# Part B: Q and K for 32 rows on four column tiles, 8 heads at a time, only V and Wo streamed

## The chip, the cores and the metric

The kernel runs on one core of a Trainium2 chip (trn2). The metric is the device time of one execution in microseconds. The core has five engines, each with its own instruction queue: TensorE (PE in the profile; PEld is its weight load), VectorE (DVE), ScalarE (ACT), GpSimd (POOL) and SyncE (SP), which only issues DMAs here. Sixteen DMA engines move data between DRAM and the on-chip SBUF; matmuls write to PSUM, from where DVE or ACT copy results to SBUF.

## The reference

Two independent computations share one launch; their outputs stand side by side in the last axis of the result. Everything is bf16.

Part A is a local attention with 32 heads of 20 over 2048 tokens of width 640: every token attends to 8 earlier tokens at a distance of 2. The change leaves it alone.

Part B is a recurrent memory transformer: 2048 tokens in 64 segments of 32, and 8 memory tokens in front of each. The output rows of the memory tokens are the memory of the next segment, so segments run one after another.

```python
for s in range(n_seg):                       # 64 segments, one after another
    xs = x[:, s * 32:(s + 1) * 32, :]
    h = concatenate([mem, xs], axis=1)       # 40 tokens x 640
    q = einsum('btd,dhe->bhte', h, Wq)       # 32 heads x 192
    k = einsum('btd,dhe->bhte', h, Wk)
    v = einsum('btd,dhe->bhte', h, Wv)
    scores = einsum('bhqe,bhke->bhqk', q, k) * scale
    p = softmax(where(mask, scores, -1e9))
    o = einsum('bhqk,bhke->bhqe', p, v)
    o = einsum('bhte,hed->btd', o, Wo)
    mem = o[:, :8, :]
    outs.append(o[:, 8:, :])
```

Each of Wq, Wk, Wv and Wo is 640 x 6144 or its transpose: 61,440 bytes on each of 128 SBUF partitions, 245,760 for all four, which is more than fits.

## The kernel before

**Order.** `part_b` first loads some of its weights (L235), runs part A (`mid`, L236) while these arrive, then loads more resident weights (L249) and runs 64 calls of `segment`. TensorE's instructions in these keep the order in which the program writes them (`manual_schedule`, L457). The other engines' orders come from the tile framework, which also puts in the waits.

**Weights.** A unit is a piece of a weight matrix. For Q, K and V it is 128 rows of the 640 times 1024 columns, 256 KB (`(m, c, dc)`, c from 0 to 5, dc from 0 to 4); for Wo it is 256 of the 6144 rows, 320 KB. `weight_plan(161000)` picks the 75 units that stay in SBUF, spread over the segment's order so that the other 39 (29 of Q, K and V, 10 of Wo; 10.9 MB) are streamed in evenly again in every segment. `get_unit` (L251) streams one: it takes the next of 8 buffers (`b_ws`) and issues the load on SP. SP issues in program order, and waits at each load until the buffer's last reader has finished.

**A segment.** `HT` holds the segment's 40 tokens, transposed: 128 partitions x 5 pieces of the 640 x 64 columns, of which 40 are used. `project` (L298) multiplies it with 1024 weight columns: for each dc two matmuls with 64 stationary columns and 512 moving columns, on two column tiles of the array (tile positions (0, 0) and (0, 64)), so their results lie on PSUM partitions 0 to 63 and 64 to 127. `project_qk` copies the result to SBUF (`sb`), and one step later its `turn` (L312) brings it back to "feature x token" by four matmuls against a selection matrix and copies it to QT or KT. That happens 6 times for Q and 6 times for K. `evacuate` (L281) gives copies out of PSUM to ACT and DVE in turns.

Heads go in two halves of 16 (t2 = 0, 1): `scores` (L322: 32 matmuls, then the softmax on DVE and ACT), `turn_p` (L352: P transposed), `values` (V stays "token x feature", so it needs no turn), `mix` (L365: P times V, 32 matmuls per half), and `project_out` (L382: 48 units of two matmuls into one accumulator `Y`). Projections stand between the steps of a half, so that softmax and copies of one step lie beside TensorE's work of another. `prep` (L285) loads the next segment's 32 tokens of x (issued on POOL) and transposes them into the other `HT`. At the end (L439 to L451) Y is copied to `Ysb` by ACT, its memory rows are transposed by TensorE and copied into the next `HT` by DVE; the next segment's first projection waits for that. Two DMAs on POOL write the output rows (L453).

Of the kernel before, what the change touches and what calls it, by code (L numbers as in the profile page):

```python
# [7 lines left out]
FP32 = mybir.dt.float32  # L8
# [141 lines left out]
def head_pieces(h):  # L150
    i = h // 2
    if h % 2 == 0:
        return [(3 * i, 0, 128), (3 * i + 1, 0, 64)]
    return [(3 * i + 1, 64, 128), (3 * i + 2, 0, 128)]


def out_units():

    return [j for t2 in range(2) for gv in range(2) for j in range(12 * t2, 12 * t2 + 12) if (j // 2) % 2 == gv]


def weight_plan(budget):

    steps = []
    for t2 in range(2):
        for m in "qk":
            for c in range(3 * t2, 3 * t2 + 3):  # L170
                steps += [((m, c, dc), 0.245) for dc in range(5)]
        steps.append((None, 1.0))
    for c in range(6):
        steps += [(("v", c, dc), 0.216) for dc in range(5)]
        if c >= 2:
            steps.append((None, 0.5))
    steps.append((None, 0.6))
    for n, j in enumerate(out_units()):
        steps.append((("o", j, 0), 0.27))
        if n == 5:  # L180
            steps.append((None, 1.1))
    steps.append((None, 1.5))
    size = lambda u: 2560 if u[0] == "o" else 2048
    total = sum(size(u) for u, _ in steps if u)
    span = sum(t for _, t in steps)
    to_stream = total - budget
    now, done, streamed = 0.0, 0, []
    for u, t in steps:
        now += t
        if u is not None and done + size(u) / 2 <= to_stream * now / span:  # L190
            streamed.append(u)
            done += size(u)
    units = [u for u, _ in steps if u]
    while total - done > budget:
        u = next(u for u in reversed(units) if u not in streamed)
        streamed.append(u)
        done += size(u)
    return [u for u in units if u not in streamed]


def part_b(ctx, tc, B_x, B_mem0, B_Wq, B_Wk, B_Wv, B_Wo, out, ident, n_seg, budget, pre, nbuf, mid):
# [7 lines left out]
    wo_v = B_Wo.rearrange("h e d -> (h e) d").rearrange("(cc p) d -> p cc d", p=128)  # L209

    def unit_src(u):
        m, c, dc = u
        if m == "o":
            return wo_v[:, 2 * c:2 * c + 2, :]
        return w_in[m][:, dc, 1024 * c:1024 * c + 1024]

    def unit_shape(u):
        return [128, 2, 640] if u[0] == "o" else [128, 1024]

    resident = weight_plan(budget)  # L220
# [3 lines left out]
    def load_resident(pool, units):  # L224
        for k, u in enumerate(units):
            t = pool.tile(unit_shape(u), BF16, name="wres_%s%d_%d" % u)
            res_engs[k % 2].dma_start(t[:], unit_src(u))
            res[u] = t[:]

    n_pre, used = 0, 0  # L230
    while n_pre < len(resident) and used < pre:
        used += 2560 if resident[n_pre][0] == "o" else 2048
        n_pre += 1
# [17 lines left out]
    def get_unit(u):  # L251
        if u in res:
            return res[u]
        t = wstream.tile([128, 1280], BF16, tag="ws")
        v = t[:].rearrange("p (a n) -> p a n", a=2) if u[0] == "o" else t[:, 0:1024]
        nc.sync.dma_start(v, unit_src(u))
        return v
# [11 lines left out]
    QTs = [cpool.tile([128, 24 * L + PADW], BF16, name=f"QT{t2}") for t2 in range(2)]  # L269
    KTs = [cpool.tile([128, 24, L], BF16, name=f"KT{t2}") for t2 in range(2)]  # L270
    Ps = [cpool.tile([128, 8 * L + PADW], BF16, name=f"P{t2}") for t2 in range(2)]
    OTs = [cpool.tile([128, 12 * L + PADW], BF16, name=f"OT{q}") for q in range(4)]
# [4 lines left out]
    sel = ident.rearrange("p (g t) -> p g t", g=2)[:, :, 0:L]  # L277
# [7 lines left out]
    def prep(s):  # L285
        HT = HTs[s % 2]
        xr = one.tile([L, Dm], BF16, tag="xr")
        lo = 0 if s == 0 else M
        n = L - lo
        if s == 0:  # L290
            nc.gpsimd.dma_start(xr[0:M, :], mem2[0:M, :])
        nc.gpsimd.dma_start(xr[M - lo:L - lo, :], x2[SEG * s:SEG * s + SEG, :])
        pt = ps_tr.tile([128, 5, L], BF16, tag="tr")
        for dc in range(5):
            nc.tensor.transpose(pt[:, dc, lo:L], xr[0:n, dc * 128:(dc + 1) * 128], ident[0:n, 0:n])  # L295
        nc.scalar.copy(HT[:, :, lo:L], pt[:, :, lo:L])

    def project(HT, m, c):  # L298
        ps = ps_acc.tile([128, 512], FP32, tag="acc")
        for dc in range(5):  # L300
            w = get_unit((m, c, dc))
            for g in range(2):
                nc.tensor.matmul(ps[64 * g:64 * g + 64, :], lhsT=HT[:, dc, :], rhs=w[:, 512 * g:512 * g + 512],  # L303
                                 start=(dc == 0), stop=(dc == 4), tile_position=(0, 64 * g))
        return ps

    def project_qk(HT, m, c):
        ps = project(HT, m, c)
        sb = qk_sb.tile([128, 512], BF16, tag="sb")
        evacuate(sb[:], ps[:])  # L310

        def turn():  # L312
            pt = ps_tr.tile([128, 4, 2, L], FP32, tag="tr")
            for j in range(4):
                nc.tensor.matmul(pt[:, j], lhsT=sb[:, 128 * j:128 * j + 128], rhs=sel, start=True, stop=True)  # L315
            t2, c0 = c // 3, 8 * (c % 3)
            dst = KTs[t2][:] if m == "k" else QTs[t2][:, 0:24 * L].rearrange("p (a n) -> p a n", n=L)
            evacuate(dst[:, c0:c0 + 8, :].rearrange("p (g j) n -> p j g n", g=2), pt[:])

        return turn  # L320

    def scores(t2):  # L322
        QT, KT = QTs[t2], KTs[t2]
        Sps = ps_at.tile([128, 8, L], FP32, tag="at")
        plist = []
        for a in range(8):
            for g2 in range(2):
                h = 16 * t2 + 2 * a + g2
                for (cc, lo, hi) in head_pieces(h):
                    plist.append((hi - lo != 128, lo, a, g2, cc - 24 * t2, hi))  # L330
# [3 lines left out]
        for n, (_, lo, a, g2, cc, hi) in enumerate(plist):  # L334
# [3 lines left out]
        t1 = one.tile([128, 8, L], FP32, tag="t1")  # L338
        nc.vector.scalar_tensor_tensor(out=t1[:], in0=Sps[:], scalar=scale,
                                       in1=mask[:].unsqueeze(1).to_broadcast([128, 8, L]),  # L340
                                       op0=ALU.mult, op1=ALU.add)
        mx = small.tile([128, 8], FP32, tag="mx")
        nc.vector.tensor_reduce(out=mx[:], in_=t1[:], axis=AX.X, op=ALU.max)
        nc.vector.tensor_tensor(t1[:], t1[:], mx[:].unsqueeze(2).to_broadcast([128, 8, L]), op=ALU.subtract)
        nc.scalar.activation(t1[:], t1[:], ACTF.Exp)
        sm = small.tile([128, 8], FP32, tag="sm")
        nc.vector.tensor_reduce(out=sm[:], in_=t1[:], axis=AX.X, op=ALU.add)
        nc.vector.reciprocal(sm[:], sm[:])
        nc.vector.tensor_tensor(out=Ps[t2][:, 0:8 * L].rearrange("p (a n) -> p a n", n=L), in0=t1[:],
                                in1=sm[:].unsqueeze(2).to_broadcast([128, 8, L]), op=ALU.mult)  # L350

    def turn_p(t2):  # L352

        pt = ps_at.tile([128, 8, 128], BF16, tag="at")
        for a in range(8):
            for g in range(2):
                nc.tensor.transpose(pt[64 * g:64 * g + 64, a, :], Ps[t2][:, L * a:L * a + 64], ident,  # L357
                                    tile_position=(0, 64 * g))
        PT = one.tile([128, 8, 2, L], BF16, tag="PT")
        src = pt[:].rearrange("p a (g n) -> p a g n", g=2)[:, :, :, 0:L]  # L360
        nc.scalar.copy(PT[:, 0:4], src[:, 0:4])
        nc.vector.tensor_copy(PT[:, 4:8], src[:, 4:8])
        return PT

    def mix(t2, PT, Vst):  # L365
        ps = [ps_at.tile([128, 12, L], FP32, tag="at", name=f"OTps{gv}") for gv in range(2)]
        plist = []
        for h in range(16 * t2, 16 * t2 + 16):
            for (cc, lo, hi) in head_pieces(h):
                gv = (cc // 4) % 2  # L370
                plist.append((hi - lo != 128, lo, cc // 8, cc % 4, gv, (h % 16) // 2, h % 2, cc, hi))
        plist.sort()
        for (_, lo, _, _, gv, a, g2, cc, hi) in plist:
            off = (cc % 4) * 128
            nc.tensor.matmul(ps[gv][lo:hi, 4 * (cc // 8 - 3 * t2) + cc % 4, :],  # L375
                             lhsT=Vst[64 * gv:64 * gv + L, cc // 8, off + lo:off + hi],
                             rhs=PT[64 * gv:64 * gv + L, a, g2, :],
                             start=True, stop=True, tile_position=(64 * gv, lo))
        for gv, cp in enumerate((nc.scalar.copy, nc.vector.tensor_copy)):
            cp(OTs[2 * t2 + gv][:, 0:12 * L].rearrange("p (a n) -> p a n", n=L), ps[gv][:])  # L380

    def project_out(Y, js):  # L382
        for j in js:
            w = get_unit(("o", j, 0))
# [8 lines left out]
    def segment(s):  # L393
# [3 lines left out]
        def step(m, c, then=None):  # L397
            nonlocal pending
            turn = project_qk(HT, m, c)
            if pending is not None:  # L400
                pending()
# [129 lines left out]
```

## Time and profile before

| | |
|---|---|
| time of three runs | median 2681.8 us (2668.77 to 2690.45) |
| profiled execution | 2675.69 us, its span 2673.7 us |
| granted TensorE clock, mean | 0.987 of full speed |
| first projection of segment 0 | 332.86 us after the span's start |
| copies of Y (L439), 64 | the first starts at 370.5 us, the last at 2663.9 us |
| streamed loads in all | 576 of Wq, 640 each of Wk, Wv and Wo |
| bytes read from DRAM | 769.93 MB |

The page lists busy time by engine, then the span in 40 slices of 67 us with the busy share of each engine in tenths and DMA's GB/s, then DMA queues, the chain of work that ended last (traced back from the last instruction, each step to what released it), the costliest groups of instructions with their mean duration and the idle time before them, and the DMA loads with the median time from issue to landing. A matmul's duration includes its way through the array, so several overlap; how fast they follow each other is read from their starts. Part A fills the first 5 slices, part B the other 35.

### The profile page before, as it was taken

How to read it: one execution, taken by the hardware profiler on the slowest of the kernel's cores; microseconds unless marked ns; L12 is line 12 of the kernel's file. 1: busy time of each engine (PE TensorE's matmuls, PEld its weight loads, DVE VectorE, ACT ScalarE, POOL GpSimd, SP SyncE). 2: the span in 40 equal slices, each digit the busy share in tenths (PEclk: the TensorE clock that was granted, in tenths of full speed). 3: DMA queues.
4: the chain of work that ended last, by engine and by line, in shares of the span. 5: the costliest groups of instructions: out<-in, count | busy, mean ns of one | idle time of the engine just before them, and what ended most of it. 6: DMA issues, size and time to landing. Idle time of an engine off the chain costs nothing.

```text
span 2673.7 us, 76688 instructions
## 1 busy us (share of the span) xinstructions
PE 2469.1 (92%) x33179; PEld 1447.6 (54%) x33194; DVE 1263.0 (47%) x2210; ACT 717.2 (27%) x1612; POOL 127.0 (5%) x259
## 2 busy tenths in 40 slices
PE   1787499999999999999999999999999999999998
PEld 0455355555555555555555555555555555555555
DVE  1566454444454444454444454444454444454444
ACT  1122122222222222222222222222222222222222
POOL 0011000000000000000000000000000000000000
PEclk9899899999999999999999999999999999999999
DMA  7777699999999999999999999999999999998997
GB/s 276 236 254 256 209 306 304 302 303 306 303 300 300 307 299 306 301 298 305 304 304 309 302 295 303 307 310 301 306 298 303 306 308 307 305 299 290 306 308 247
DMA packets 493426, 788.15 MB, mean 295 GB/s; under 512 B 46376, under 2 KB 240752, under 8 KB 493088
## 3 DMA queue, kind: packets, MB, share of 16 engines
q1 hardware_dynamic: 474224, 740.76, 84.3%
q0 software_dynamic: 12160, 31.93, 3.5%
q10 hardware_dynamic: 6704, 10.57, 1.1%
q8 instruction: 259, 4.24, 0.6%
q14 instruction: 79, 0.65, 0.1%
HBM read 769.93 MB, written 13.15 MB: 293 GB/s over the span
## 4 chain that ended last, share of the span: by engine, by line
PE 82%; DMA 5%; ACT 1%; DVE 1%; issue 0%; SPq 0%; POOLq 0%; POOL 0%; ACTq 0%; DVEq 0%
PE ps L303 51%; PE Y L389 13%; PE pt L315 7%; PE Sps L335 4%; DMA t<-in_B_Wo_dram 4%; PE OTps L375 2%; PE pt L357 2%; PE pt L448 1%; ACT Ysb L439 1%; DMA K<-a_kv_scr 1%; PE pt L295 1%; DVE HT L451 0%; DMA wres_o<-in_B_Wo_dram 0%; DVE K L98 0%; DMA a_kv_scr<-qkv 0%
## 5 line engine op out<-in xcount | busy, mean ns | idle before, releaser
L303 PEld LDWEIGHTS <-HT 128*64 128x64 bf16 x11520 | 566.2, 109 | 467.7 <-DVE HT L451 24.3
L283 DVE CAST sb<-ps 128x512 bf16<-128x512 f32 x704 | 485.8, 690 | 530.3 <-PE ps L303 522.1
L303 PE MATMUL ps<-t,HT 128*64 128x512 bf16 x3712 | 714.1, 387 | 0.0
L303 PE MATMUL ps<-wres_q,HT 128*64 128x512 bf16 x2688 | 426.0, 385 | 25.6 <-DVE HT L451 18.4
L303 PE MATMUL ps<-wres_k,HT 128*64 128x512 bf16 x2560 | 387.4, 383 | 0.0
L389 PEld LDWEIGHTS <-OT 128*64 128x64 bf16 x6144 | 341.8, 110 | 74.0 <-issue 11.0
L303 PE MATMUL ps<-wres_v,HT 128*64 128x512 bf16 x2560 | 373.7, 380 | 0.0
L389 PE MATMUL Y<-wres_o,OT 128*64 128x320 bf16 x3584 | 318.4, 299 | 0.0
L315 PEld LDWEIGHTS <-sb 128*128 128x128 bf16 x3072 | 142.7, 100 | 316.9 <-issue 211.9
L283 ACT CAST QT<-pt 128x320 bf16<-128x320 f32 x384 | 163.6, 426 | 409.6 <-PE pt L315 409.6
L389 PE MATMUL Y<-t,OT 128*64 128x320 bf16 x2560 | 264.6, 300 | 6.8 <-DMA t<-in_B_Wo_dram 6.2
L283 ACT CAST KT<-pt 128x320 bf16<-128x320 f32 x384 | 163.6, 426 | 393.2 <-PE pt L315 393.2
L315 PE MATMUL pt<-ident,sb 128*128 128x80 bf16 x3072 | 244.2, 205 | 0.0
L283 DVE CAST Vst<-ps 128x512 bf16<-128x512 f32 x256 | 176.6, 690 | 129.7 <-PE ps L303 129.7
L451 DVE CAST HT<-pt 128x40 bf16<-128x40 f32 x63 | 12.6, 200 | 345.2 <-PE pt L448 345.2
L283 ACT CAST Vst<-ps 128x512 bf16<-128x512 f32 x128 | 75.0, 586 | 269.0 <-PE ps L303 269.0
L380 DVE CAST OT<-OTps 128x480 bf16<-128x480 f32 x128 | 84.2, 658 | 126.0 <-PE OTps L375 126.0
L335 PEld LDWEIGHTS <-QT 128*64 128x64 bf16 (+1 forms) x4096 | 108.8, 110 | 21.2
L335 PE MATMUL Sps<-KT,QT 128*64 128x40 bf16 (+1 forms) x4096 | 118.7, 186 | 0.0
L439 ACT CAST Ysb<-Y 128x320 bf16<-128x320 f32 x64 | 27.3, 426 | 292.0 <-PE Y L389 292.0
L380 ACT CAST OT<-OTps 128x480 bf16<-128x480 f32 x128 | 71.6, 560 | 119.7 <-PE OTps L375 117.2
L65 PE MATMUL pq<-wqkv,xT 128*128 128x480 bf16 x320 | 88.1, 404 | 16.8 <-ACT xT L60 10.0
(72 smaller groups left out, 1543.7 us busy)
## 6 DMA issues: line engine op xcount, KB each, us to landing
t<-in_B_Wo_dram SPq DMA_DIRECT2D x640, 320.0 KB, 5.0
t<-in_B_Wk_dram SPq DMA_DIRECT2D x640, 256.0 KB, 4.3
t<-in_B_Wv_dram SPq DMA_DIRECT2D x640, 256.0 KB, 3.9
t<-in_B_Wq_dram SPq DMA_DIRECT2D x576, 256.0 KB, 4.3
K<-a_kv_scr SPq DMA_DIRECT2D x16, 1280.0 KB, 6.3
V<-a_kv_scr POOLq DMA_DIRECT2D x16, 1280.0 KB, 8.6
a_kv_scr<-qkv POOLq DMA_DIRECT2D x16, 320.0 KB, 5.1
wres_q<-in_B_Wq_dram SPq DMA_DIRECT2D x11, 256.0 KB, 5.4
```

The lines of the kernel that those rows point to most:

```text
L65: nc.tensor.matmul(pq[:], lhsT=xT[:, c, :], rhs=wqkv[:, c, g * 480:(g + 1) * 480], start=(c == 0), stop=(c == 4))
L283: (nc.scalar.copy if copies["n"] % 2 else nc.vector.tensor_copy)(dst, src)
L295: nc.tensor.transpose(pt[:, dc, lo:L], xr[0:n, dc * 128:(dc + 1) * 128], ident[0:n, 0:n])
L303: nc.tensor.matmul(ps[64 * g:64 * g + 64, :], lhsT=HT[:, dc, :], rhs=w[:, 512 * g:512 * g + 512], start=(dc == 0), stop=(dc == 4), tile_po ...
L315: nc.tensor.matmul(pt[:, j], lhsT=sb[:, 128 * j:128 * j + 128], rhs=sel, start=True, stop=True)
L335: nc.tensor.matmul(Sps[64 * g2:64 * g2 + 64, a, :], lhsT=QT[lo:hi, L * cc:L * cc + 64], rhs=KT[lo:hi, cc, :], start=(g2 not in seen), stop ...
L357: nc.tensor.transpose(pt[64 * g:64 * g + 64, a, :], Ps[t2][:, L * a:L * a + 64], ident, tile_position=(0, 64 * g))
L375: nc.tensor.matmul(ps[gv][lo:hi, 4 * (cc // 8 - 3 * t2) + cc % 4, :], lhsT=Vst[64 * gv:64 * gv + L, cc // 8, off + lo:off + hi], rhs=PT[64 ...
L380: cp(OTs[2 * t2 + gv][:, 0:12 * L].rearrange("p (a n) -> p a n", n=L), ps[gv][:])
L389: nc.tensor.matmul(Y[64 * g:64 * g + 64, :], lhsT=OTs[2 * t2 + gv][:, L * c:L * c + 64], rhs=w[:, i, 320 * g:320 * g + 320], start=(j == 0 ...
L439: nc.scalar.copy(Ysb[:], Y[:])
L448: nc.tensor.matmul(pt[lo:lo + c1 - c0, dc, :], lhsT=Ysb[:, c0 - 320 * g:c1 - 320 * g], rhs=ident[:, 64 * g:64 * g + M], start=True, stop=True,
```

## The change

Four things change together, in part B alone.

1. Q and K are computed for 32 rows instead of 64: the 8 memory tokens and the first 24 tokens of x, on four column tiles of 32 columns, each with 384 of a unit's 1536 weight columns (`project32`). `turn` takes 3 matmuls.
2. Rows of x, unlike the memory rows, are known from the start, so Q and K of the last 8 tokens of a segment can be computed at any time. `XL` holds these of four segments (32 rows), and `project_late` computes Q and K of them for one group of heads at once. A segment calls it for group s % 4, so each group comes up every fourth segment; all four groups are computed ahead of segment 0. The results lie in `LT`; POOL copies the 8 columns that a segment needs behind the other 32 (`project_qk`).
3. Heads go in four groups of 8 (g = 0 to 3), so that all tiles of a step are half as large. V and Y still run on two column tiles with 64 rows. Wo's rows are dealt out so that a unit is one contiguous piece of 480 KB.
4. All of Q and K stays in SBUF. Only V (units of 384 KB) and Wo are streamed, and `stream_plan(45000)` keeps 12 of their 36 units resident: 24 are streamed per segment, in the order V 0/0 to 0/4, V 1/0 to 1/3, V 2/0 to 2/3, Wo 0 to 3, V 3/1, V 3/4, Wo 5, 8, 10, 12, 15. There are 5 stream buffers of 480 KB instead of 8 of 320 KB.

The diff, cut (lines that only go are left out where the listing above has them):

```diff
+GROUPS = 4
...
+    wo_v = B_Wo.rearrange("h e d -> (h e) d").rearrange("(i p r) d -> p i (r d)", p=128, r=3)
...
+    resident = [(m, g, dc) for g in range(GROUPS) for m in "qk" for dc in range(5)] + stream_plan(budget)
...
-        t = wstream.tile([128, 1280], BF16, tag="ws")
-        v = t[:].rearrange("p (a n) -> p a n", a=2) if u[0] == "o" else t[:, 0:1024]
+        t = wstream.tile([128, 1920], BF16, tag="ws")
+        v = t[:, 0:unit_cols(u)]
         nc.sync.dma_start(v, unit_src(u))
...
+    XL = cpool.tile([128, 5, 32], BF16, name="XL")
+    LT = {m: [cpool.tile([128, 12, 32], BF16, name=f"L{m}{g}") for g in range(GROUPS)] for m in "qk"}
...
+        nc.gpsimd.dma_start(xr[0:SEG, :], x2[SEG * s:SEG * s + SEG, :])
+        if late:
+            nc.gpsimd.dma_start(xr[SEG:L, :], x2[SEG * (s + 4) - M:SEG * (s + 4), :])
...
+        nc.scalar.copy(HT[:, :, M:L], pt[:, :, 0:SEG])
+        if late:
+            i = (s + 3) % 4
+            nc.vector.tensor_copy(XL[:, :, M * i:M * i + M], pt[:, :, SEG:L])
...
+    def project32(X, m, g):
+
+        ps = ps_acc.tile([128, 384], FP32, tag="acc")
+        for dc in range(5):
+            w = get_unit((m, g, dc))
+            for j in range(4):
+                nc.tensor.matmul(ps[32 * j:32 * j + 32, :], lhsT=X[:, dc, 0:32], rhs=w[:, 384 * j:384 * j + 384],
+                                 start=(dc == 0), stop=(dc == 4), tile_position=(0, 32 * j))
+        sb = qk_sb.tile([128, 384], BF16, tag="sb")
         evacuate(sb[:], ps[:])
...
+    def turn(sb, dst):
+        pt = ps_tr.tile([128, 3, 4, 32], FP32, tag="tr")
+        for c in range(3):
+            nc.tensor.matmul(pt[:, c], lhsT=sb[:, 128 * c:128 * c + 128], rhs=ident, start=True, stop=True)
+        evacuate(dst.rearrange("p (j c) n -> p c j n", c=3), pt[:])
...
+    def project_qk(s, m, g):
+        T = (QTs if m == "q" else KTs)[g % 2]
+        i = s % 4
+        nc.gpsimd.tensor_copy(tokens(T)[:, :, 32:L], LT[m][g][:, :, M * i:M * i + M])
+        sb = project32(HTs[s % 2], m, g)
+        return lambda: turn(sb, tokens(T)[:, :, 0:32])
+
+    def project_late(m, g):
+        sb = project32(XL, m, g)
+        return lambda: turn(sb, LT[m][g][:])
+
+    def values(s, g):
+        HT = HTs[s % 2]
+        Vst = work.tile([128, 2, 384], BF16, tag="Vst")
+        pv = [ps_acc.tile([128, 384], FP32, tag="acc", name=f"pv{c}") for c in range(2)]
+        for dc in range(5):
+            w = get_unit(("v", g, dc))
+            for c in range(2):
+                for gv in range(2):
+                    n = 768 * c + 384 * gv
+                    nc.tensor.matmul(pv[c][64 * gv:64 * gv + 64, :], lhsT=HT[:, dc, :], rhs=w[:, n:n + 384],
+                                     start=(dc == 0), stop=(dc == 4), tile_position=(0, 64 * gv))
+        for c in range(2):
+            evacuate(Vst[:, c, :], pv[c][:])
+        return Vst
...
+    def segment(s):
+        last = s + 1 == n_seg
+        tq, tk, V, PT = {}, {}, {}, {}
+        tq[0] = project_qk(s, "q", 0)
+        tk[0] = project_qk(s, "k", 0)
+        while late:
+            late.pop(0)()
+        tq[0]()
+        tq[1] = project_qk(s, "q", 1)
+        tk[0]()
+        tk[1] = project_qk(s, "k", 1)
+        tq[1]()
         scores(0)
+        V[0] = values(s, 0)
+        tk[1]()
+        tq[2] = project_qk(s, "q", 2)
         scores(1)
+        tk[2] = project_qk(s, "k", 2)
+        tq[2]()
+        PT[0] = turn_p(0)
+        V[1] = values(s, 1)
+        tk[2]()
+        mix(0, PT[0], V[0])
+        tq[3] = project_qk(s, "q", 3)
+        scores(2)
+        tk[3] = project_qk(s, "k", 3)
+        tq[3]()
+        PT[1] = turn_p(1)
+        V[2] = values(s, 2)
+        tk[3]()
+        mix(1, PT[1], V[1])
+        Y = ps_y.tile([128, 320], FP32, tag="y")
+        project_out(Y, 0)
+        scores(3)
+        PT[2] = turn_p(2)
+        if not last:
             prep(s + 1)
+        V[3] = values(s, 3)
+        mix(2, PT[2], V[2])
+        project_out(Y, 1)
+        PT[3] = turn_p(3)
+        project_out(Y, 2)
+        mix(3, PT[3], V[3])
+        if not last:
+            late.append(project_late("q", s % 4))
+        project_out(Y, 3)
         Ysb = work.tile([128, 320], BF16, tag="Ysb")
         nc.scalar.copy(Ysb[:], Y[:])
+        if not last:
+            late.append(project_late("k", s % 4))
...
             nc.vector.tensor_copy(HTn[:, :, 0:M], pt[:])
+            late.pop(0)()
...
+    prep_first()
     prep(0)
     with tc.manual_schedule(engines={mybir.EngineType.PE}):
+        for g in range(GROUPS):
+            for m in "qk":
+                project_late(m, g)()
         for s in range(n_seg):
             segment(s)
...
-    part_b(ctx, tc, B_x, B_mem0, B_Wq, B_Wk, B_Wv, B_Wo, out, ident, n_seg=n_seg, budget=161000, pre=110000, nbuf=8,
+    part_b(ctx, tc, B_x, B_mem0, B_Wq, B_Wk, B_Wv, B_Wo, out, ident, n_seg=n_seg, budget=45000, pre=110000, nbuf=5,
```

The new `scores`, `turn_p` and `mix` work on 8 heads with 16, 8 and 24 matmuls (before: 16 heads with 32, 16 and 32), and `project_out(Y, g)` takes four Wo units of three pairs of matmuls each. `prep_first` loads the memory and the last 8 tokens of the first three segments. After the change the matmul of `project32` is on L310, V's on L345, the copy of Y on L467 and the streamed load on L243.

## The prediction

> **What bounds the kernel now.** I read the page from its top: engines, slices, chain; then the timeline of TensorE and the waits inside one steady stretch.
>
> ```profile
> PE 2469.1 (92%) x33179; PEld 1447.6 (54%) x33194; DVE 1263.0 (47%) x2210; ACT 717.2 (27%) x1612; POOL 127.0 (5%) x259
> ...
> PE   1787499999999999999999999999999999999998
> ...
> DMA  7777699999999999999999999999999999998997
> ...
> PE 82%; DMA 5%; ACT 1%; DVE 1%; issue 0%; SPq 0%; POOLq 0%; POOL 0%; ACTq 0%; DVEq 0%
> ```
>
> TensorE is full from the sixth slice on, which is where part B's 64 segments run, and it is 82% of the chain. DMA is as full by share, yet 5% of the chain: both could be the limit, so the DMA digits need a second look. The 64 copies of Y (L439) start between 370.5 and 2663.9 us: a period of 2293.4/63 = 36.40 us per segment. The chain's blocks of 72 Y matmuls lie 36.20 apart where no DMA piece stands between them, so 0.2 us a segment is DMA. Around the periods: 370.5 us to the first Y copy, 9.8 us after the last.
>
> ```profile
> 1030.43 0.38 PE L303 MATMUL ps<-t,HT 128*64 128x512 bf16 x2
> 1030.65 0.38 PE L303 MATMUL ps<-wres_q,HT 128*64 128x512 bf16 x2
> 1030.96 0.32 PE L315 MATMUL pt<-ident,sb 128*128 128x80 bf16 x4
> 1031.21 0.62 PE L303 MATMUL ps<-wres_q,HT 128*64 128x512 bf16 x4
> 1031.67 0.38 PE L303 MATMUL ps<-t,HT 128*64 128x512 bf16 x2
> 1031.88 0.60 PE L303 MATMUL ps<-wres_q,HT 128*64 128x512 bf16 x4
> 1032.41 0.32 PE L315 MATMUL pt<-ident,sb 128*128 128x80 bf16 x4
> ```
>
> Starts, not durations, give the price. Pairs on two column tiles start 0.216 us apart (1030.43, 1030.65; single instructions show the second of a pair 3 to 4 ns after the first): two matmuls for the price of one. Before a turn the gap is 0.31, so each change of tile shape costs about 0.10.
>
> ```profile
> SPq L256 <- PE ps L303: 425.4, 622, 1.9
> SPq L256 <- PE Y L389: 105.3, 159, 1.4
> ...
> PE Y L389 <- DMA t<-in_B_Wo_dram: 1.3, 4, 0.5
> ```
>
> These are waits in 1000:2000. The queue that issues weights spends most of its time waiting until TensorE has read a buffer; TensorE waits for a weight 1.3 us in 1000. The stream is held back by its eight buffers, not by bandwidth: 303 GB/s at a share of 0.92 there, but 386 GB/s in full 5 us stretches of the first load (15 to 50 us).
>
> **TensorE's work per segment.** Q and K: 60 pairs of 512 columns x 0.216 = 12.95 us go. 40 groups of four with 384 columns come, and 10 more for the late tokens. No row shows four column tiles of 32. From below: a group streams 384 columns, 384/512 x 0.216 = 0.162. From above: one pair after another, 0.324. Weight loads could decide as well: busy time over count is 49 ns on L303, 27 ns on L335, 15 ns on L375, so four take 0.06 to 0.20. I take 0.162, as the 64x64 matmuls of L375 start four within about 10 ns; 50 x 0.162 = 8.10, a gain of 4.85.
>
> The Trainium skill speaks against this ("TensorE: Matmul & The Clock Gate", Part 3, measured speedups): three column tiles of 32 gave 2.38 times one, not three. Scaling my group by 3/2.38 would make it 0.204 and the sum below 2.1 us larger per segment; no run here shows it.
>
> Turns: 12 x 4 starts 0.040 apart (1.92) become 10 x 3 of 128 columns, 0.056 apart like the 128-column pairs of L357 (1.68): -0.25. Equal: V (30 x 0.216 against 40 x 0.162), scores, P's turns and Y by count; about 40 changes of tile shape in both. Mix goes from 64 to 96 smaller matmuls: between -0.3 and +0.3 by L375's two halves, I take 0. The end of a segment: TensorE waits 0.52 for the Y copy and 0.29 for HT; the late K projection and the late Q turn, already counted, now run there. About 0.27 is left: -0.54. New wait: scores(1) follows K's turn by one projection of 0.9 us, but the evacuation of that turn is queued on DVE behind softmax and V's copy: 0 to 0.6, I take 0.5. Period by TensorE alone: 36.20 - 4.85 - 0.25 - 0.54 + 0.5 = 31.1.
>
> Copies cover themselves: by the page's forms (690 ns for 512, 490 for 320, so 0.56 for 384 on DVE, 0.48 on ACT) a segment holds about 18 us of DVE and 11 of ACT. POOL gets eight copies of 128x12x8; no row shows one. The affine selects took 0.21 and 0.29, so 2 to 3 us per segment beside four DMA issues of 0.5 (prep loads x in two pieces now, a segment early in POOL's order); from zero to 1 us each nothing waits, since the copies for a segment's first four tiles stand ahead of the previous segment's output DMAs in POOL's order, and these wait for Ysb.
>
> **What is late next: the stream.** 12 of 36 V and Wo units stay, so 15 V units (384 KB) and 9 Wo units (480 KB) are streamed: 10.3 MB per segment against 10.9. Bandwidth is enough at 31 us: 333 GB/s. The window is not: five buffers, and a load is issued only when the unit five places earlier has been read.
>
> ```profile
> t<-in_B_Wo_dram SPq DMA_DIRECT2D x640, 320.0 KB, 5.0
> t<-in_B_Wk_dram SPq DMA_DIRECT2D x640, 256.0 KB, 4.3
> ...
> wraw<-in_A_wqkv_dram SPq DMA_DIRECT2D x1, 2400.0 KB, 9.8
> ```
>
> These medians hold queueing. Loads whose predecessor landed 2.2 to 2.6 us after their issue took 3.55 us for 256 KB; at 400 GB/s (landings of queued loads 0.64 apart) 0.65 of it is transfer, so the lag is 2.9. Then 480 KB is 1.23 + 2.9 = 4.1 us, 384 KB 0.98 + 2.9 = 3.9. Bounds of the lag: 2.3, from wraw and K (1280 KB, 6.3 us) put on a line; 3.65, from the median 4.3.
>
> In out-projection 0 all four Wo units are streamed, right behind four streamed V units. The second Wo unit takes the buffer of V group 2's first: issued 0.38 after that group starts, landed at 4.5. TensorE wants it after V 1.62, K's turn 0.27, mix 0.30, a change 0.10 and one unit of Wo 0.41 (0.136 per pair): at 2.7. Late 1.8; the third and fourth come 1.23 apart and cover 0.41 each: 0.82 late each. Together 3.5. V group 1: its fourth streamed unit is fourth in line after V group 0's first (0.38 + 3.9 + 3 x 0.98 = 7.2) and wanted at 6.3 (V 1.62, a turn 0.27, projections 2 x 0.91, scores 0.55 and their wait 0.5, a turn 0.27, P's turn 0.32, three units 0.97): 0.9, with its third unit 1.0. Other places (Y1, Y2, V0) and the spread of landings, about 0.5 either way of which only lateness counts: 0.6. Sum 5.1; period 31.1 + 5.1 = 36.2. The gain comes back as waits for weights.
>
> The skill has a smaller lag ("DMA: Bandwidth & Descriptors", anatomy of one DMA): 2.0 us plus bytes at 436 GB/s, for DMAs from GpSimd. 480 KB would be 3.1, and the period some 1.3 us shorter. The page's 320 KB loads took 5.0 where that rule gives 2.75, so the trace decides.
>
> **Before the first segment.** Eight late projections and their turns run in series: projection 0.91, drain and hand-over 0.25, copy 0.48, turn 0.27: 1.9 each, 15 us. Nothing covers them: ACT, which copies them, is busy issuing resident loads until about 332 us, as it is before (first projection at 332.86). The load itself is about the same (7.0 MB after part A against 6.4). Bounds 8 (overlapped) to 20 (the first pairs now start at 332.86 and 333.29, 0.43 apart, at half the clock).
>
> **Sum.** Profiled execution 2675.7 (span 2673.7 and 2.0 around it): +15 and 63 x (36.2 - 36.4) = -13 make 2678; the median of the runs is 6.1 higher: 2684. Each 0.1 us of period is 6.3 us.
>
> **Rivals.** One: the stream keeps up better. At a lag of 2.3 the two late places shrink by 0.6 each: 35.0, 2608; with no stall 31.1, 2363. For it: before, the stream hardly stalls TensorE. Against: eight buffers then, and never eight streamed units in 4 us of TensorE's work. Two, the slower side: the groups of four are not one stream. If they go as two pairs (0.324), +8.1, of which the V wait of 1.0 comes back: 43.3, 3131. At 0.20 (weight loads) +1.9, of which some 0.4 comes back: 37.7, 2778. It decides from 0.170 per group on: +1% of 2681.8 is 0.39 us over 50 groups. For it: no such row. Against: pairs cost one. Three: the lag under load is 3.65, both places 0.75 later: 37.7, 2778.
>
> **Numbers.** Forecast (35.4 to 37.0: 2634 to 2734) 0.50; rival one below that 0.22; two 0.16; three 0.12. 1% (27 us) is what I count as told from no change. Of the forecast's half 0.11 lies below 2655 and 0.12 above 2709: faster 0.33, same 0.27, slower 0.40. The range leaves out 0.1 on each side, rival one under 34.7 and rivals two and three over 38.8: 2590 to 2850.
>
> **What would show it.** L310's group starts 0.16 apart: TensorE's part holds; 0.2 or more: rival two. PE waits for t<-in_B_Wo_dram near 3.5 us a segment, for t<-in_B_Wv_dram near 1: the window holds; under 2 in all: rival one. Y copies 36.2 apart, and the first near 384 us. DMA digits fall to 8, and PE's too. A long wait of scores for POOL would break the sum in a place I gave nothing.

## The result, and the profile after

| | before | after |
|---|---|---|
| median of 4 runs each, us | 2686.12 (2668.77 to 2691.47) | 2901.43 (2896.8 to 2906.1) |
| ratio | | 1.081, 95% interval 1.076 to 1.087 |
| profiled execution (span), us | 2675.7 (2673.7) | 2906.1 (2904.3) |
| mean granted TensorE clock | 0.987 | 0.906 |
| first Y copy (L439, now L467), us | 370.5 | 393.7 |
| period of the 64 Y copies, us | 36.40 | 39.77 |
| from the last Y copy to the end, us | 9.9 | 4.8 |

The change made the kernel 8% slower; 2684 was forecast and 2850 was the upper end of the range. Nearly all of the miss is the period: 39.77 against 36.2, 63 times, is 225 us. The start adds 8 (393.7 against the 370.5 + 15 of the sum; the 384 among the forecast's signs does not fit its own sum). The shorter tail takes 5 back, and another 11 go because the median lies 4.7 below the profiled execution, where the sum had put it 6.1 above.

The page of the changed kernel, first busy time, slices and chain, at its end the loads (KB each, median us from issue to landing):

```profile
PE 2410.6 (83%) x40633; PEld 1523.6 (52%) x40633; DVE 1222.6 (42%) x3110; ACT 738.0 (25%) x1811; POOL 284.0 (10%) x833
...
PE   1788588888888888888888888888888988888887
...
PEclk9899689998998999989998989998899899989899
DMA  6777387787787777778777777777777777877777
...
PE 61%; DMA 30%; DVE 3%; issue 1%; ACT 0%; SPq 0%; POOL 0%; POOLq 0%; ACTq 0%; DVEq 0%
...
t<-in_B_Wv_dram SPq DMA_DIRECT2D x960, 384.0 KB, 4.9
t<-in_B_Wo_dram SPq DMA_DIRECT2D x576, 480.0 KB, 5.0
```

TensorE and the DMA engines are both less busy than before (8 and 7 where 9 and 9 stood), so neither looks short of capacity: they wait for each other, and loads are now 30% of the chain. The line that was not looked for is PEclk: 8s among the 9s right to the end, where the steady part of the kernel before has a granted clock of 1.00 (its line stands below).

The waits in 1000:2000, some 25 segments (us in total, times, longest us):

```profile
PE Y L414 <- DMA t<-in_B_Wo_dram: 91.1, 75, 3.2
PE pv L345 <- DMA t<-in_B_Wv_dram: 36.6, 44, 2.3
PE Sps L362 <- DVE KT L273: 8.7, 25, 0.4
...
SPq L243 <- PE pv L345: 489.0, 254, 7.2
SPq L243 <- PE Y L414: 195.5, 223, 1.8
```

Divided by 1000/39.77: 3.6 us per segment for Wo and 1.45 for Wv, and nothing for POOL. These are the waits that were forecast (3.5 and 1.0 to 1.6). So 31.1 + 5.1 should have held, and it did not: something that is no wait is missing. The timeline of TensorE around one such wait has it (start, duration, x count, idle before):

```profile
1006.97 0.60 PE L414 MATMUL Y<-t,OT 128*64 128x320 bf16 x6 [0.93 <-DMA t<-in_B_Wo_dram]
1010.25 1.01 PE L414 MATMUL Y<-t,OT 128*64 128x320 bf16 x6 [2.68 <-DMA t<-in_B_Wo_dram]
1011.41 1.01 PE L414 MATMUL Y<-t,OT 128*64 128x320 bf16 x6 [0.15 <-DMA t<-in_B_Wo_dram]
...
1040.39 1.79 PE L310 MATMUL ps<-wres_q,HT 128*32 128x384 bf16 x20
1042.12 0.56 PE L362 MATMUL Sps<-KT,QT 128*64 128x40 bf16 x16
1042.60 1.00 PE L310 MATMUL ps<-wres_k,HT 128*32 128x384 bf16 x20
1043.53 0.34 PE L319 MATMUL pt<-ident,sb 128*128 128x128 bf16 x3
```

The same six Y matmuls take 0.60 before the long wait and 1.01 after it. A projection (20 matmuls, five groups of four) hands over to the next shape 0.93 after its start, which is 5 x 0.162 and a change of shape: four column tiles do run as one stream. But 2 us earlier the like projection took 1.73. The clock record has it at 0.5 from 1008.0 to 1014.9 and from 1038.8 to 1042.2, and the windows view (length, PE busy with its count, then the other engines, granted clock, DMA share, GB/s) agrees:

```profile
1008.10:1014.80 6.70, 4.40 (x49) 3.12 (x50) 1.43 (x5) 0.91 (x3) 1.17 (x4) 0.50 0.94 339
1015.00:1038.00 23.00, 21.17 (x401) 13.38 (x398) 9.89 (x28) 6.33 (x15) 2.33 (x8) 1.00 0.71 239
```

Busy time between the first and the last Y copy gives the account per segment (first the kernel before, then the changed one):

```profile
370.52:2663.86 2293.34, 2235.38 (x31180) 1302.65 (x31180) 1089.13 (x2016) 635.49 (x1448) 92.25 (x187) 1.00 0.92 303
393.66:2899.48 2505.82, 2156.16 (x38342) 1370.15 (x38337) 1045.56 (x2894) 652.50 (x1636) 243.49 (x746) 0.91 0.77 264
```

2156.16/63 = 34.22 us busy and 5.55 idle per segment. By the clock record 7.15 us of each segment pass at half clock. TensorE is busy in 6.21 of these, and half of that, 3.1 us, is an estimate of what the same work would not have needed at full clock.

### The profile page after: what moved, and what is told of

Same layout as the page of the kernel before. It is cut to its first block, busy times and chain, and to the rows that moved or that the text cites. A ratio compares the mean times of both kernels' runs of the same rounds, so it can differ in the third digit from the quotient of the medians.

```text
span 2904.3 us, 92166 instructions
## 1 busy us (share of the span) xinstructions
PE 2410.6 (83%) x40633; PEld 1523.6 (52%) x40633; DVE 1222.6 (42%) x3110; ACT 738.0 (25%) x1811; POOL 284.0 (10%) x833
## 4 chain that ended last, share of the span: by engine, by line
PE 61%; DMA 30%; DVE 3%; issue 1%; ACT 0%; SPq 0%; POOL 0%; POOLq 0%; ACTq 0%; DVEq 0%
PE ps L310 17%; PE pv L345 15%; DMA t<-in_B_Wo_dram 14%; PE Y L414 13%; DMA t<-in_B_Wv_dram 13%; PE pt L319 4%; PE Sps L362 3%; PE OTps L398 3%; PE pt L384 2%; DMA K<-a_kv_scr 1%; DVE sb L273 1%; DMA a_kv_scr<-qkv 1%; PE pq L65 1%; DVE K L98 1%; PE lgp L103 1%
## 5 line engine op out<-in xcount | busy, mean ns | idle before, releaser
L345 PE MATMUL pv<-t,HT 128*64 128x384 bf16 x3840 | 428.8, 349 | 94.5 <-DMA t<-in_B_Wv_dram 93.6
L345 PEld LDWEIGHTS <-HT 128*64 128x64 bf16 x5120 | 312.0, 122 | 257.8 <-issue 125.8
L273 DVE CAST sb<-ps 128x384 bf16<-128x384 f32 x383 | 213.0, 556 | 387.7 <-PE ps L310 387.5
L310 PEld LDWEIGHTS <-HT 128*32 128x32 bf16 x10240 | 236.5, 98 | 149.1 <-DVE HT L480 22.4
L310 PE MATMUL ps<-wres_q,HT 128*32 128x384 bf16 x5120 | 266.1, 339 | 11.5 <-DVE HT L480 11.5
L310 PE MATMUL ps<-wres_k,HT 128*32 128x384 bf16 x5120 | 261.5, 334 | 0.0
L273 DVE CAST Vst<-pv 128x384 bf16<-128x384 f32 x256 | 140.7, 549 | 268.5 <-PE pv L345 268.5
L319 PE MATMUL pt<-ident,sb 128*128 128x128 bf16 x1938 | 211.7, 224 | 5.1 <-ACT sb L273 5.1
L273 ACT CAST sb<-ps 128x384 bf16<-128x384 f32 x263 | 125.7, 478 | 346.9 <-PE ps L310 346.9
L345 PE MATMUL pv<-wres_v,HT 128*64 128x384 bf16 x1280 | 202.7, 423 | 0.0
```

Source lines behind the costliest of these rows:

```text
L273: (nc.scalar.copy if copies["n"] % 2 else nc.vector.tensor_copy)(dst, src)
L310: nc.tensor.matmul(ps[32 * j:32 * j + 32, :], lhsT=X[:, dc, 0:32], rhs=w[:, 384 * j:384 * j + 384], start=(dc == 0), stop=(dc == 4), tile_ ...
L319: nc.tensor.matmul(pt[:, c], lhsT=sb[:, 128 * c:128 * c + 128], rhs=ident, start=True, stop=True)
L345: nc.tensor.matmul(pv[c][64 * gv:64 * gv + 64, :], lhsT=HT[:, dc, :], rhs=w[:, n:n + 384], start=(dc == 0), stop=(dc == 4), tile_position= ...
```

## The experiments

The theory: five buffers cannot carry a run of eight streamed units, TensorE waits for weights, and the waits halve its clock, which makes the other work longer. The rivals: the stream's bytes per second are the limit; the four-column work itself pulls the clock down; another wait or a late step was missed. Runs without an interval are single runs, beside 2678.5 to 2679.2 of the kernel before.

**No stream** (2349.9 us).

```
         if u in res:
             return res[u]
+        return res[{"v": ("v", 3, 0), "o": ("o", 4, 0)}[u[0]]]
```

> This kernel leaves out the 24 streamed loads of a segment: where a V or Wo unit would be loaded, a resident unit of the same kind is read instead, so the output is not the reference's, and no DMA of weights runs after the first load. Theory (waits for weights, and the half clock that follows them, are all that is wrong): TensorE alone, 31.1 us per segment, granted clock 1.00 from the first segment on, 394 + 63 x 31.1 + 5 = 2358 us (2330 to 2390). Rival 'the groups of four pull the clock down': clock stays near 0.91 and the period near 31.1 / 0.91 = 34.2, 2550 us. Rival 'something in the copies or in the late projections was missed': clock 1.00, but a period well over 32.

```profile
379.01:2343.28 1964.27, 1930.04 (x38342) 1269.94 (x38337) 1032.31 (x2894) 653.89 (x1637) 245.34 (x746) 1.00 0.02 6
```

The period is 31.18 with a clock of 1.00: the sum for TensorE's own work was right to 0.1 us, and groups of four do not lower the clock. Of the 31.18, 30.64 are busy and 0.54 idle. Against that the changed kernel has 5.01 more idle and 3.58 more busy, and these two are the whole 8.6 us that the stream costs it.

Where they lie shows in the starts of TensorE's steps in both traces (from one step's start to the next one's, mean of 62 segments). V group 1 takes 1.9 us longer than without the stream and out-projection 0 takes 4.5 longer. V group 3, which does not wait, takes 1.2 longer, and all other steps together 1.0. So 6.4 us arise in the two places of the waits, and 2.2 in steps elsewhere, nearly all of them behind the waits, where TensorE mostly works and is slow.

**Work in place of the waits** (2759.3 us).

```
+    def keep_busy(pairs):
+        pt = ps_tr.tile([128, 384], FP32, tag="tr")
+        for _ in range(pairs):
+            for gv in range(2):
+                nc.tensor.matmul(pt[64 * gv:64 * gv + 64, :], lhsT=HTs[0][:, 0, :], rhs=res[("q", 0, 0)][:, 0:384],
+                                 start=True, stop=True, tile_position=(0, 64 * gv))
...
+            if g == 1 and dc in (2, 3):
+                keep_busy(4)
...
+            if g == 0 and a > 0:
+                keep_busy(7)
```

> All loads as in the changed kernel, the output too; added are matmuls whose result nobody reads, 7 pairs of 384 columns (1.13 us) ahead of the second, third and fourth Wo unit of out-projection 0 and 4 pairs (0.65 us) ahead of the third and fourth V unit of group 1: 4.7 us per segment, about the 5.07 that TensorE waits there. Theory (the waits cost 5 us and the half clock after them another 3.5): TensorE is busy in the waits, the clock stays near 1.00, and in spite of 4.7 us more work the period FALLS from 39.8 to 36.2 (31.1 + 4.7 + 0.4), 2680 us (2660 to 2720). Rival 'the stream itself delivers a segment's 10.3 MB no faster than in 39.8 us': the added work fills the waits and the period stays 39.8, 2900 us. Rival 'the clock falls for another reason than the waits': period 39.8 or longer at a clock near 0.9, 2900 to 3150.

```profile
383.64:2752.69 2369.05, 2262.25 (x41996) 1526.26 (x41991) 1032.32 (x2894) 653.56 (x1637) 245.00 (x746) 1.00 0.80 279
```

TensorE does 35.91 us of work per segment, 5.3 more than without the stream, and the segment is 2.2 us shorter than in the changed kernel. The loads are the same ones, so the stream was not at its limit, and it is the clock that came back, from 0.91 to 1.00. V group 1 and out-projection 0 take nearly as long as in the changed kernel (1.7 and 4.4 us more than without the stream), but V group 3 takes 1.75 us as without the stream: what was saved is the slow work behind the waits. The time is 39 us above the upper end of what was expected, and the period 37.6 rather than 36.2: the added work came to 5.3 rather than 4.7, and 1.0 us of waits for weights is left.

**Other residents, same buffers** (2683.5 us).

```
-    resident = [(m, g, dc) for g in range(GROUPS) for m in "qk" for dc in range(5)] + stream_plan(budget)
+    keep = ([("v", 2, dc) for dc in (2, 3, 4)] + [("v", 3, dc) for dc in (1, 2, 3, 4)] +
+            [("o", i, 0) for i in (2, 5, 7, 8, 9, 13)])
+    resident = [(m, g, dc) for g in range(GROUPS) for m in "qk" for dc in range(5)] + keep
```

> Same five buffers and 23 streamed units of 10.0 MB rather than 24 of 10.3, but other ones: resident are V 2,2 to 2,4, V 3,1 to 3,4 and Wo 2, 5, 7, 8, 9, 13, so that the run of eight streamed units from V group 2 to Wo 3 becomes five of nine. Output as the reference. Theory (five buffers against a burst of streamed units): waits for weights fall from 5.1 to 2.3 us per segment, most of them left in V group 1, period 33.8 at full clock and up to 1.7 more if one half-clock stretch of 3.4 us stays in each segment: 2530 to 2640 us, 2560 likeliest. Rival 'bytes per second': the period follows the bytes, 39.8 x 10.0/10.3 = 38.7, 2835 us.

Period 36.31: 3.2 us of waits per segment rather than 5.0 (their main place is now V, 53.7 us in 1000:2000 against 33.3 for Wo), and 1.1 lost to half clock rather than 3.1. The direction and the bytes rival are settled (2835 was its price), but the size was missed, by 44 us above the upper end: 0.9 us more of waits stayed than had been worked out.

**Six buffers** (2702.4 us).

```
-    resident = [(m, g, dc) for g in range(GROUPS) for m in "qk" for dc in range(5)] + stream_plan(budget)
+    resident = [(m, g, dc) for g in range(GROUPS) for m in "qk" for dc in range(5)] + stream_plan(budget)[:-2] + [("o", 14, 0)]
...
-    part_b(ctx, tc, B_x, B_mem0, B_Wq, B_Wk, B_Wv, B_Wo, out, ident, n_seg=n_seg, budget=45000, pre=110000, nbuf=5,
+    part_b(ctx, tc, B_x, B_mem0, B_Wq, B_Wk, B_Wv, B_Wo, out, ident, n_seg=n_seg, budget=45000, pre=110000, nbuf=6,
```

> Six stream buffers rather than five; to make room, Wo unit 13 is streamed too (25 units, 10.8 MB, 5% more bytes). Output as the reference. Theory (window): waits fall from 5.1 to about 3.2 us per segment, period 34.5 at full clock plus 1 to 2 for half-clock stretches: 36, 2665 us (2600 to 2740). Rival 'bytes per second': 5% longer, 41.7, 3025 us.

Period 36.78, with 5% more bytes: 3.3 us of waits, 1.8 lost to half clock. The bytes rival falls a second time, and one buffer more gives back 3.0 of the 8.6 us.

**All four weights streamed, evenly** (2499.5 us).

```
-    resident = [(m, g, dc) for g in range(GROUPS) for m in "qk" for dc in range(5)] + stream_plan(budget)
+    streamed = [("k", 0, 2), ("k", 1, 2), ("k", 2, 2), ("k", 3, 1), ("q", 0, 1), ("q", 1, 2), ("q", 2, 1), ("q", 3, 4),
+                ("v", 0, 1), ("v", 0, 2), ("v", 0, 4), ("v", 1, 0), ("v", 1, 4), ("v", 2, 0), ("v", 2, 3),
+                ("v", 3, 0), ("v", 3, 3), ("v", 3, 4)] + [("o", i, 0) for i in (0, 3, 6, 11, 12, 14)]
+    resident = [u for u in [(m, g, dc) for g in range(GROUPS) for m in "qkv" for dc in range(5)] +
+                [("o", i, 0) for i in range(16)] if u not in streamed]
```

> Five buffers and 24 streamed units as in the changed kernel (15 to 18 of 384 KB, the rest of 480 KB), but taken from all four weights and evenly along TensorE's order: 8 units of Wq and Wk, 10 of Wv, 6 of Wo. The late projections read a streamed unit of Wq or Wk again, so a segment loads 10.6 MB rather than 10.3. Output as the reference. Theory (not too few bytes per second and not too few buffers as such, but streamed units that are wanted in bursts): waits for weights 0.3 to 1.2 us per segment rather than 5.1, no window idle enough for the clock to drop, period 31.6 to 32.5, 2375 to 2450 us, 2400 likeliest. Rival 'the stream delivers at most the 300 GB/s seen so far': 10.6 MB in 35.3 us, 2610 us or more.

(The bytes are 10.8 MB: 18 x 384 KB, 6 x 480 KB, and two second readings.) This undoes one part of the change, "only V and Wo streamed". Its waits in 1000:2000, some 30 segments:

```profile
PE pv L349 <- DMA t<-in_B_Wv_dram: 17.5, 34, 1.4
PE Y L418 <- DMA t<-in_B_Wo_dram: 15.3, 36, 1.7
PE ps L314 <- DMA t<-in_B_Wq_dram: 5.5, 9, 1.0
```

With five buffers, 24 streamed units and more bytes, the waits fall from 5.1 to 1.4 us per segment, none over 1.7, the granted clock between the Y copies is 1.00 and the stream moves 328 GB/s. The time is 49 us and the period, 33.41, 0.9 above the upper end of what was expected, so the waits were sized too low again. But with the same number of buffers and more bytes 6.4 of the 8.6 us are gone: it is the burst that five buffers cannot carry.

**The kernel before with five buffers** (2904.3 us; the edit is nbuf=8 to nbuf=5).

> The kernel before with five stream buffers rather than eight, nothing else: its units are 256 and 320 KB, streamed evenly along all four weights. Output as the reference. Theory (what counts is bytes in flight against the lag of a load, here 1.3 to 1.6 MB rather than 2.0 to 2.5): the stream falls behind, 10.9 MB at some 270 GB/s, period 40.7 and 1 to 2 for half clock: 42, 3030 us (2900 to 3150), waits for weights at Q, K, V and Wo alike. Rival 'evenly spread, five buffers are enough': 36.4 to 37, 2680 to 2720 us.

```profile
365.12:2892.34 2527.22, 2331.12 (x31180) 1373.65 (x31180) 1089.60 (x2016) 635.92 (x1448) 92.59 (x187) 0.99 0.86 275
```

Its period is 40.11 and its time that of the changed kernel, by another road: 3.1 us idle per segment, but the clock stays at 0.99 in the steady part. Its waits come in many small pieces (Wo 61 times in 1000:2000, 0.67 us on average). So five buffers are too few for its smaller units even when evenly spread. Two parts of the expectation failed: 0.6 us per segment is lost to half clock rather than 1 to 2, and the waits are not alike (40.8 of 54.3 us are for Wo, none is listed for K). Waiting in small pieces cost far less clock here than the changed kernel's long waits cost it.

**Made gaps** (2524.8 us): the kernel without stream, and in out-projection 0 of segment s TensorE waits for s mod 8 copies on ScalarE.

```
+    def gap(copies):
+        pt = ps_tr.tile([128, 384], FP32, tag="tr")
...
+        lhs, rhs = HTs[0][:, 0, :], res[("q", 0, 0)][:, 0:384]
+        for half in range(2):
+            for gv in range(2):
+                nc.tensor.matmul(pt[64 * gv:64 * gv + 64, :], lhsT=lhs, rhs=rhs, start=True, stop=True,
+                                 tile_position=(0, 64 * gv))
+            if half == 0:
+                for k in range(copies):
+                    nc.scalar.copy(z[:], pt[:])
+                rhs = z[:]
...
+            if a == 2 and copies:
+                gap(copies)
```

> The kernel without streamed loads (it leaves them out as before, resident units stand in), with one made gap in each segment: after the second Wo unit of out-projection 0, TensorE waits for s mod 8 copies of 384 columns on ScalarE (0.48 us each, in a row), then goes on; two pairs of unread matmuls stand on each side. The gaps should be none, 0.75, 1.2, 1.7, 2.2, 2.7, 3.1, 3.6 us in eight segments each. Theory, from the records of the changed kernel (full clock is lost at the end of a 3.41 us window of a fixed grid in which TensorE idled 1.42 us or more, and is given back after one full window without idle): no drop for gaps up to 1.2, in most segments at 1.7 and 2.2, in all at 2.7 and above; mean period 34.8, 2575 us. Rival (The Trainium skill, 'TensorE: Matmul & The Clock Gate', has the clock fall after more than 3.4 us of idle): drops at 3.6 alone, period 33.8, 2510 us.

The timeline after four copies (first three lines) and, one segment later, after five:

```profile
1032.92 0.51 PE L414 MATMUL pt<-z,HT 128*64 128x384 bf16 x2 [2.10 <-ACT z L418]
1033.17 1.86 PE L433 MATMUL Y<-wres_o,OT 128*64 128x320 bf16 x12
1034.77 0.80 PE L363 MATMUL Sps<-KT,QT 128*64 128x40 bf16 x16
...
1068.58 0.35 PE L414 MATMUL pt<-z,HT 128*64 128x384 bf16 x2 [2.62 <-ACT z L418]
1068.74 1.01 PE L433 MATMUL Y<-wres_o,OT 128*64 128x320 bf16 x12
1069.55 0.55 PE L363 MATMUL Sps<-KT,QT 128*64 128x40 bf16 x16
```

The windows view of the 3.4 us behind each gap (the granted clock is the third number from the end):

```profile
1033.00:1036.40 3.40, 3.40 (x45) 2.79 (x46) 0.71 (x3) 0.23 (x1) 0.48 (x2) 0.50 0.02 5
1068.70:1072.10 3.40, 3.40 (x63) 2.73 (x60) 1.56 (x6) 0.96 (x3) 1.00 (x2) 1.00 0.02 5
```

The shorter gap halves the clock (1.86 against 1.01 for 12 matmuls), the longer one does not, and that in 7 of 8 and 8 of 8 segments. Clock changes lie on a fixed grid of 3.413 us; over this grid the gap of 2.10 fell into one window in those 7 segments and was split in the eighth (0.97 and 1.14), and the gap of 2.62 was split each time, in the segment shown into 1.15 and 1.46. Over all 56 gaps: no window at full clock with at most 1.54 us of idle was followed by a drop, every one with 1.97 or more was.

The price can be read off too. A segment with four copies takes 33.83 us without a drop and some 35.26 with one, so the drop costs 1.4 us; with five copies, a longer gap and no drop, it takes 34.25. After seven copies the clock stays at half for two windows and the price is some 2.4 (37.64 where the gap alone would make 35.3).

So the theory's mechanism is shown; its threshold of 1.42, taken from the changed kernel's record, was too low for clean gaps, and fewer drops than counted on made the period 34.15 rather than 34.8. By its time this run lies nearer to the rival (33.8); what decides against the rival is where the drops came. In the changed kernel's own record the windows that lead to a drop have 1.37 to 3.1 us of idle, while some with up to 1.8 lead to none; why the border is not sharp there is open. "TensorE: Matmul & The Clock Gate" of the Trainium skill (Part 1, and the part on oscillation) gives the same window, 3413 ns and free-running, and warns of idle gaps over about 3.4 us; the runs here have the clock fall after 2.1.

**The start** (2871.2 us): the turns of the late projections before segment 0 come one projection later.

```
-                project_late(m, g)()
+                turns.append(project_late(m, g))
+                if len(turns) == 2:
+                    turns.pop(0)()
+        turns.pop()()
```

> The changed kernel with one edit before segment 0: the turn of a late projection is issued after the next late projection, not at once. Output as the reference. Theory (serial chain, at half clock because TensorE idles 0.6 us of every 2.9): the eight late projections take 9 to 13 us rather than 22.8, at full clock by the third one, and the first Y copy comes at 381 to 385 rather than 393.7; the rest unchanged, 2890 us (2875 to 2910). Rival 'the half clock at the start comes from the idle time before, whatever the order': 14 to 19 us.

Three starts, TensorE's timeline; the changed kernel, then the one with six buffers, then this one:

```profile
333.58 1.79 PE L310 MATMUL ps<-wres_k,XL 128*32 128x384 bf16 x20
335.96 0.50 PE L319 MATMUL pt<-ident,sb 128*128 128x128 bf16 x3 [0.59 <-ACT sb L273]
336.39 1.79 PE L310 MATMUL ps<-wres_q,XL 128*32 128x384 bf16 x20
```

```profile
331.54 1.00 PE L310 MATMUL ps<-wres_q,XL 128*32 128x384 bf16 x20
333.12 0.34 PE L319 MATMUL pt<-ident,sb 128*128 128x128 bf16 x3 [0.59 <-ACT sb L273]
333.39 1.00 PE L310 MATMUL ps<-wres_k,XL 128*32 128x384 bf16 x20
```

```profile
332.20 1.00 PE L310 MATMUL ps<-wres_k,XL 128*32 128x384 bf16 x20
333.13 0.34 PE L319 MATMUL pt<-ident,sb 128*128 128x128 bf16 x3
333.40 1.00 PE L310 MATMUL ps<-wres_q,XL 128*32 128x384 bf16 x20
```

In the changed kernel one late projection takes 2.81 to 2.88 us, since the clock is at 0.5 (from 322.0 to 356.1): each cycle holds 0.6 us of idle, and the full windows of the grid in this stretch hold 0.64 to 0.94 until a last one with 0.42 brings the clock back. The kernel with six buffers happened to be granted full clock at 330.1 us, after a window with 0.58 us of idle, and took 1.85 to 1.91, the forecast 1.9. With the turns moved the cycle is 1.2 and no wait shows; from 324.4 to segment 0's first projection at 336.5 it takes 12.2 us rather than 22.8. The rival (14 to 19 us) falls. The first Y copy came at 374.2, earlier than expected; 6.3 us of that are no part of the edit, since the first late projection began at 324.4 and not at 330.7. The time, 4 us below the range, holds another 15 us from a period of 39.53, which the edit does not touch.

**Both edits together, with five and with six buffers** (medians of four runs). The six-buffer kernel streams one Wo unit more and has its own even list.

> The two edits that gained together: five buffers with 24 units streamed from all four weights in turn (as measured alone: period 33.4) and the late projections before segment 0 with each turn one projection later (as measured alone: about 11 us). Output as the reference. Expected by theory: 2499 less 11, 2488 us (2470 to 2500), 0.926 of the kernel before. If the two gains are one and the same (both only keep the clock up at the start), 2499.

> As the kernel with five buffers run beside it, but six buffers and one Wo unit more streamed (25 units, 11.3 MB a segment with the late projections' second reading, rather than 10.8). Output as the reference. Theory (a wait for a weight is a matter of how early its load can be issued): waits 0.3 to 0.9 us per segment, period 32 to 32.9, 2395 to 2455 us. Rival (with bursts gone, bytes per second are the limit, at the 329 GB/s seen with five): period 34.3, 2540 us, slower than with five.

2487.3 us with five, 0.924 of the kernel before (0.921 to 0.928); 2433.9 with six, 0.907 (0.904 to 0.909). The page and the steady stretch of the second:

```profile
PE   0787769999999999999999999999999999999998
...
PEclk9889979999999999999999999999999999999999
DMA  7677779999999999999999999999999999999998
```

```profile
373.84:2424.24 2050.40, 1959.59 (x38342) 1283.42 (x38338) 1036.21 (x2894) 654.67 (x1636) 243.76 (x746) 1.00 0.98 352
```

Its period is 32.55, 1.4 above TensorE alone, and it moves 352 GB/s, so the 329 seen with five buffers was not the limit either. TensorE and DMA are now full together (busy shares of 0.96 and 0.98). How much the DMA engines have left is not shown: while the first weights arrive they moved 402 GB/s in this run.

## Why the prediction was wrong

- **TensorE's work, 31.1.** Right: 31.18 without the stream. Groups of four start 0.162 apart, as taken. By the prediction's estimate the 2.38 of the Trainium skill ("TensorE: Matmul & The Clock Gate", Part 3) would have made the sum 2.1 us longer, and the run does not have it. Rival two falls.
- **New wait of scores, 0.5, and POOL's copies at nothing.** 0.35 per segment (8.7 us in 25 segments), and the copies took 0.27 us each with nobody waiting.
- **The window, 5.1 per segment.** Right in place and kind, and the listed waits match (3.6 for Wo and 1.45 for Wv), but that match is in part luck: at half clock TensorE asks for weights later, and what it then works more slowly it waits less. By starts the two places cost 6.4 us, V group 1 1.9 and out-projection 0 4.5, where 1.0 and 3.5 were forecast; in segments whose step ran at full clock throughout (56 and 9 of 62) they cost 1.7 and 3.8. Rival one falls. Rival three (1.75 and 4.25) may be true in part; alone it gives 37.7. A slip in the working: a lag 0.9 us shorter takes 0.9 off each place, some 1.8 and not 1.3.
- **"Period 31.1 + 5.1 = 36.2": the step that failed.** It put waits beside work whose duration stays the same. Here 3.58 us of busy time came on top, and the clock was in no term, rival or bound of the period. Instruction by instruction against the run without the stream, 2.6 of it are work that passed more slowly at half clock (the estimate of 3.1 was too high) and 0.9 are the ends of the last matmuls ahead of each wait, which nothing overlaps and the profile counts as busy. Put by place, the miss of 3.6 is 2.2 in steps outside the two places, for which the sum had nothing, 1.3 for the places themselves (6.4 against 5.1) and 0.1 in TensorE's own work.
- **The start, 15 us.** Wrong by the same cause: 22.8 at half clock, though the prediction had even seen the first pairs at half clock and used that only as a bound (20). At full clock the term is right (1.85 to 1.91 against 1.9).
- **What would show it.** L310's starts and both waits came as written and the DMA digits fell (to 7 rather than 8), and yet the time did not come: the list had no line for the granted clock.

The time of the change thus splits into a gain that is there (36.40 to 31.18 per segment by TensorE alone), 5.0 us given back as idle time, and 3.6 given back again as longer busy time. It was lost to one of its four parts: with the same five buffers and the loads spread over all four weights, 33.41 is left.

## What to carry to other kernels

When waits are forecast in an engine's order, ask whether they come in one place: a made gap of 2.1 us cost another 1.4 by the clock here, one of 3.6 another 2.4, while in the kernel before with five buffers, whose waits come in small pieces, the clock cost 0.6 us per segment in all. Plan what stays resident by where the loads are wanted, not by weight: a stream with few buffers needs its loads evenly along the consumer's order. Put the granted clock into the list of things that a profile must show.

## What the runs showed of the hardware

The granted clock knows two values in these steady stretches, 1.0 and 0.5, and changes on a fixed grid of 3.413 us. A window with about half of it idle was enough to halve the clock (border between 1.54 and 1.97 us with made gaps), so whether a gap of 2.1 us costs anything depends on where it falls. Coming back took a window with little idle: of the 76 recovering windows in the changed kernel's steady part 75 have at most 0.11 us and one has 0.29. The border is not settled: at the starts windows with 0.42 and 0.58 us brought the clock back, while a serial chain whose windows held 0.64 to 0.94 stayed at half clock for its 22.8 us, and four windows without idle in the changed kernel were not followed by full clock at once.
